# Half as many plain output products between two gating stages, six seven-product groups at the end, and a weight load moved to another queue

## The chip, the cores and the metric

The kernel runs on one core of a Trainium2 chip. The metric is device time in microseconds: the median of several executions on the chip. The engines of the core are TensorE (PE, matrix products; PEld is its weight load), VectorE (DVE), ScalarE (ACT), GpSimd (POOL) and SyncE (SP). SP does nothing here but issue DMAs; ACT issues some too, on a queue of its own. "PSUM bank" below is one of the eight banks of 128×512 f32 in which PE leaves its sums.

## The reference, cut to what matters

Two sub-layers with residuals, on 2048 tokens of width 1024, all in bfloat16:

```python
h  = x + A(layernorm(x))          # segmented attention, 32 heads, 4 segments of 512 tokens
h2 = h + B(layernorm(h))

def B(x, w_in, w_sp, b_sp, w_out):
    z  = gelu(x @ w_in)                            # 2048 x 3584
    z1 = z[..., :1792]
    z2 = layernorm(z[..., 1792:])
    g  = einsum('ts,bsf->btf', w_sp, z2) + b_sp    # mixes tokens: w_sp is 2048 x 2048
    return (z1 * g) @ w_out                        # w_out is 1792 x 1024
```

The change lies in B, behind z1 and z2: in the token mixing ("gating"), the product with `z1`, and the product with `w_out`.

## The kernel before

Every instruction is recorded by a small scheduler, `_Recorder` (L34–241): one list per engine (`pe`, `act`, `dve`, `pool`, `sp`), each in program order, with waits found from the memory cells that an instruction reads and writes. So the order of the Python text is the order on each engine; an engine whose next instruction must wait holds all that stands behind it. All instructions are emitted by one line (`emit`, L210), so a group in the profile is told by its tiles. SBUF is a hand-laid arena (`tens(name, ..., offset)`): two tiles at one address are in use one after the other, and the later waits for the earlier.

The stages, by time in the profiled execution: attention, to about 330 us; z2 = layernorm of the second half of the gelu; z1 to 489.9 (`z1_step`, L1199), kept transposed (features on partitions, tokens along the free axis) in `Z1T`; then four stages that the change touches:

1. `gate(0)` (L1087), 489.9 to 574.6: g and z1·g for tokens 0 to 1023.
2. The w_out units, 574.8 to 623.0: 16 `out_unit`s (L1179). Each makes 128 tokens × 512 columns of the output by 14 matmuls (1792 = 14 × 128) and adds them to `h`, which an earlier stage left in the output's DRAM and `fin_load` brings back.
3. `gate(1)`, 623.0 to 707.8: the same as 1 for tokens 1024 to 2047.
4. The end groups, 707.8 to 753.0: w_out for tokens 1024 to 2047, four groups.

Stages 1, 3 and 4 use a product scheme with seven block products where the plain one has eight (Winograd's form). For gating, w_sp's part is cut in blocks b11, b12, b21, b22, each 512 tokens × 1024; the sums t1 = b12−b11, t2 = b22−t1, t3 = b22−b12, t4 = b21−t2 are made once (`sp_sum`); on the other side four sums of z2 blocks (`s_sum`, tile `ss`, also `SS`) are made for each of the seven feature groups g. One group is seven products of eight matmuls 128×512, in the order t2, t1, b11 of a later group (`p1`), t3, b21 of the next (`p2`), t4, b22. DVE turns the banks into results: `stt` (bank × scale + an addend; tiles `tmp_u`, `tmp_s1b`, `vb`) and `out` (times `Z1T`, into `z1T` or `z1x`). ACT copies p1's bank (`copy1`), POOL adds the row of b_sp to it twice (`tmp_s1b<-tmp_s,brow`). An end group has the same form with seven matmuls per product: `y_sum`s take the place of `s_sum`s, and w_out is cut in 2×2 (the pieces `OB`, sums `ob_sum`).

Scales: the scheme works in f16, so b blocks are multiplied by a power of two, SC[0], when cast from bf16 to f16 (`sp_half` on DVE, a whole block; `sp_part` on ACT, a quarter). The results of gate 1 (Z1X) carry a scale YS, w_out's f16 copies a scale SCW; `scale_y` and `scale_w` work them out among the units from sums of squares, and INVO undoes both.

The preparation of gate 1 lies among the units: 16 DMA transposes on SP's queue (`sp_load`, each 256 KB; tiles `b11r` to `b22r`), the casts, the sums t1 to t4, the first three `ss`. w_out's first half of columns (`WO0`, two DMAs of 896 KB) comes on SP before gate 0; the second half (`WO1`) comes on ACT's queue at the head of the units, beside the transposes. For the end groups the second half comes once more, to `Z1T[:, :, 0:512]`, after the transposes.

Of the kernel before, what the change touches and what calls it, by code (L numbers as in the profile page):

```python
# [33 lines left out]
class _Recorder:  # L34


    def __init__(self, nc):
        self.nc = nc
        self.ops = {k: [] for k in ENGS}
        self.dmas = []  # L40
        self.known = {k: ({f: -1 for f in ENGS}, 0) for k in ENGS}
        self.cells = {}
        self.banks = {}
        self.space = {}
        self.cache = {}
        self.dma_sems = {}
        self.out_dmas = []
        for k in ENGS:
            setattr(self, k, _Eng(self, k))
# [37 lines left out]
    def record(self, eng, name, args, kw, dma=None):  # L87
# [94 lines left out]
        if dma is not None:  # L182
# [4 lines left out]
            key = (aps_out[0] is sb, sb.tensor.name, int(sb.offset))  # L187
# [8 lines left out]
    def emit(self):  # L196
# [9 lines left out]
        def run(eng, e):  # L206
            for op in self.ops[eng]:
                for o in op.waits:
                    e.wait_ge(o.dma if o.dma is not None else sems[o.eng], o.val)
# [49 lines left out]
def bass_sequential_preLN__memory_aug_infini_attn__mixer_gmlp__prompt_kernel(  # L259
# [126 lines left out]
    SQ = b3("sq", [128, 16], F32)  # L386
# [6 lines left out]
    TW, YS, INVY, SCW, INVO = [b3(k, [128, 1], F32) for k in ("tw", "ys", "invy", "scw", "invo")]  # L393
    SQY = tens("sqy", [128, 28], F32, 768)
    BSQ = tens("bsq", [128, 2], F32, 896)
# [6 lines left out]
    WO1 = [tens("w_out1%d" % i, [128, 7, 512], BF16, o * K) for i, o in enumerate((30, 4))]  # L402
    WO0H = [tens("w_out0h%d" % i, [128, 7, 512], F16, o * K) for i, o in enumerate((54, 198))]
    FIN2 = tens("fin2", [128, 4, 2, 2, 512], BF16, 14 * K)
    OT4 = [[tens("ot%d%d" % (i, k), [128, 512], F32, (o + 2 * k) * K) for k in range(4)] for i, o in enumerate((38, 118))]
# [533 lines left out]

    def scale_of(k, n, b):  # L940
# [4 lines left out]
        if k:  # L945
            dve.reciprocal(TOP[:], TOT[:])
        else:
            pool.tensor_tensor(TOP[:], TOT[:], MHZ[:], ALU.pow)
# [53 lines left out]
    at(37, pool.tensor_copy, SQB[:, 0:16], SQ[:])  # L1002
# [6 lines left out]
    at(20, pool.tensor_copy, SQB[:, 0:14], SQZ[:])  # L1009
    at(25, scale_of, 1, 14, None)  # L1010
    at(25, scale_end, 1)
    for k in range(8):
        at(26 + k, wz_half, k // 2, k % 2)
    for k in range(4):
        at(28 + 2 * k, hn_sum, 1, 1 + k // 2, k % 2)
    for k in (1, 2, 3, 4):
        at(35 + k, sz_sum, 0, k)
# [4 lines left out]
    for it in todo:  # L1022
# [6 lines left out]
        if it == (0, 12):  # L1029
            sp_norm_load(0)  # L1030
            sp_norm_load(1)
# [28 lines left out]

    SUMS = {"t1": ("b12", "b11"), "t2": ("b22", "t1"), "t3": ("b22", "b12"), "t4": ("b21", "t2")}
# [25 lines left out]
    def gate(pr, seam=lambda: None, mid=lambda: None, each=lambda g, k: None):  # L1087
        inv, zo = (INV[0], Z1T) if pr == 0 else (INVY, Z1X)
        t1, t2 = slice(1024 * pr, 1024 * pr + 512), slice(1024 * pr + 512, 1024 * pr + 1024)
        s1, s1b1, s1b2, u2, u3 = (TMP[k][:] for k in ("s1", "s1b1", "s1b2", "u2", "u3"))  # L1090

# [19 lines left out]
        def c11(g):  # L1111
            stt(VB[:], g % 3, BROW[0][:])
            out(VB[:], g, 0, t1)
# [6 lines left out]
        if not pr:  # L1120
            p1(2)
        seam()
        p2(0)
        c11(0)
        for g in range(7):
# [6 lines left out]
            ss(4, g)  # L1132
# [3 lines left out]
            if 1 - pr <= g <= 3:  # L1136
                p1(g + 2)
# [12 lines left out]
            stt(VB[:], bc, u3)  # L1150
            out(VB[:], g, 1, t2)
            if not g:
                ss(1, 1)
                ss(2, 1)
            if g < 6:
# [6 lines left out]
            stt(VB[:], bb, s1b1)  # L1162
            out(VB[:], g, 1, t1)
# [3 lines left out]
            stt(VB[:], bc, u2)  # L1167
            out(VB[:], g, 0, t2)
# [10 lines left out]
    def out_unit(u, wsl, q=sp):  # L1179
        tc, lo, w = u  # L1180
        b = next_bank()
        mm8(PS[:, b, 0:w], lambda i: Z1T[:, i, tc * 128:(tc + 1) * 128], wsl, n=14)
        fin = fins[u]
        dve.tensor_tensor(fin[:, 0:w], fin[:, 0:w], PS[:, b, 0:w], ALU.add)
# [7 lines left out]
    wout = B_w_out.rearrange("(c p) n -> p c n", p=128)  # L1192
# [55 lines left out]
    on(1, 7, scale_of, 0, 16, None)  # L1248
    on(2, 2, scale_end, 0)
    for k, g, r in (("b11", 6, 3), ("b12", 6, 3), ("b22", 8, 3), ("b21", 12, 3)):  # L1250
# [17 lines left out]
    units = [(tc, 0, 512) for tc in range(6)] + [(tc, 512, 512) for tc in range(8)] + [(tc, 0, 512) for tc in (6, 7)]  # L1268
# [9 lines left out]
    def z1_norm(g, k):  # L1278
        for h in range(k and 2):
            r, o = 2 * g + (k > 2), 1024 + 512 * h  # L1280
            if k != 2:
                act.activation(bank(7), Z1T[:, r, o:o + 512], ACTF.Square, accum_out=SQY[:, 2 * r + h:2 * r + h + 1])

    gate(0, seam, mid, z1_norm)
    pool.tensor_copy(TW[:], TOT[:])
    fin_load(units[0], act)
    fin_load(units[1], act)
    for k in ("b11", "b12", "b22", "b21"):
        for j in range(4):
            sp_load(1, k, j)  # L1290
    brow_load(1, act)
    for i in range(2):
        act.dma_start(WO1[i][:], wout[:, 7 * i:7 * i + 7, 512:D])
    pool.tensor_copy(SQB[:], SQY[:])

    def total(n):
        b = next_bank()
        pe.matmul(PS[:, b, 0:n], ONES[:], SQB[:, 0:n], start=True, stop=True)
        dve.tensor_reduce(out=TOT[:], in_=PS[:, b, 0:n], axis=mybir.AxisListType.X, op=ALU.add)
        dve.tensor_single_scalar(TOT[:], TOT[:], 1e-30, ALU.max)  # L1300

    def power(o):
        pool.tensor_tensor(TOP[:], TOT[:], MHZ[:], ALU.pow)
        dve.tensor_single_scalar(TOP[:].bitcast(I32), TOP[:].bitcast(I32), 0x7F800000, ALU.bitwise_and)
        dve.tensor_single_scalar(o[:], TOP[:], 8192.0, ALU.mult)

    def scale_y():
        total(28)
        pool.tensor_single_scalar(TW[:], TW[:], float(2 * T * FH), ALU.mult)
        for k in range(2):  # L1310
            pool.tensor_tensor(TW[:], TW[:], BSQ[:, k:k + 1], ALU.add)
        pool.tensor_tensor(TOT[:], TOT[:], TW[:], ALU.mult)
        power(YS)
        dve.tensor_tensor(INVY[:], INV[0][:], YS[:], ALU.mult)
        for k in range(2):
            act.activation(BROW[k][:], BROW[k][:], ACTF.Copy, scale=YS[:])

    def brow_sq():
        for k in range(2):
            act.activation(BH["t4"][:, k, :], BROW[k][:], ACTF.Square, scale=float(np.sqrt(2.0)), accum_out=BSQ[:, k:k + 1])  # L1320

    def wo_norm(k):
        v = (WO0, WO1)[k // 4][k // 2 % 2].rearrange("p c n -> p (c n)")[:, 1792 * (k % 2):1792 * (k % 2) + 1792]
        act.activation(BH["t4"][:, 0:4, :].rearrange("p c n -> p (c n)")[:, 0:1792], v, ACTF.Square, accum_out=SQY[:, k:k + 1])

    def scale_w():
        total(8)
        power(SCW)
        dve.tensor_tensor(INVO[:], YS[:], SCW[:], ALU.mult)
        dve.reciprocal(INVO[:], INVO[:])  # L1330

    for n, u in enumerate(units):
        if n + 2 < 16:
# [3 lines left out]
        if 1 <= n <= 8:  # L1337
            wo_norm(n - 1)
        if n == 6:
            brow_sq()  # L1340
        if n == 7:
            scale_y()
        if n == 10:
            pool.tensor_copy(SQB[:, 0:8], SQY[:, 0:8])
        if n == 1:
            sp_half("b11")
        if n == 4:
            sp_half("b12")
            sp_sum("t1")
        if n == 6:  # L1350
            sp_half("b22")
            sp_sum("t3")
        if n == 8:
            sp_sum("t2")
        if n == 10:
            sp_half("b21")
            sp_sum("t4")
        if n == 12:
# [175 lines left out]
```

## Time and profile before

| | us |
|---|---|
| median of 5 runs | 755.01 (754.09 to 756.37) |
| profiled execution | 754.75 |
| its span in the profile | 753.0 |
| PE busy | 743.7 (99%) |
| DVE busy | 556.9 (74%) |
| ACT busy | 421.7 (56%) |
| POOL busy | 295.7 (39%) |
| gate 0 / units / gate 1 / end groups | 84.7 / 48.4 / 84.8 / 45.2 |

The span is from the first to the last instruction that the profile shows; the execution's time has 1.75 us around it. Matmuls are pipelined, so a row such as "1.89 … x8" is longer than the step from one product to the next; the step is what counts. In the windows view each engine's busy time stands with its number of instructions. A group's row ends with the idle time ahead of it and what released it.

### The profile page before, as it was taken

The page shows a single profiled execution, that of the slowest core. Times are in us where ns is not written, and L with a number is a line of the kernel's source. Part 1 is how long each engine was busy: PE and PEld are TensorE (multiplying, and loading weights), DVE is VectorE, ACT ScalarE, POOL GpSimd, SP SyncE. Part 2 cuts the span into 40 slices and gives each one's busy share as a digit, 9 for nine tenths or more (in the row PEclk, how much of TensorE's full clock was granted, in tenths as well). Part 3 has the DMA queues.
Part 4 walks back from the last instruction along what each step waited for, and adds up shares of the span by engine and source line. Part 5 has one row for each costly group of instructions (what it writes and reads, how often), then busy time and mean ns, then how long its engine had stood idle before and what let it go on. Part 6 is the DMA issues. An engine that isn't in the chain of part 4 may idle for free.

```text
span 753.0 us, 13441 instructions
## 1 busy us (share of the span) xinstructions
PE 743.7 (99%) x5401; PEld 358.8 (48%) x5470; DVE 556.9 (74%) x1013; ACT 421.7 (56%) x519; POOL 295.7 (39%) x450
## 2 busy tenths in 40 slices
PE   8999999999999999999999999999999999999998
PEld 3445455555554445545554444444444444444444
DVE  5586589768975576677986796997885385989776
ACT  6777877787777767325994879733231355300000
POOL 2565456555654334010039888622220001222342
PEclk9999999999999999999999999999999999999999
DMA  9654556444523331669650027330019960001211
GB/s 297 175 166 80 93 82 128 100 78 89 115 67 73 122 88 44 161 183 262 196 164 0 1 45 138 56 98 1 0 26 140 261 203 30 0 1 44 77 50 57
DMA packets 136783, 75.09 MB, mean 100 GB/s; under 512 B 98064, under 2 KB 126480, under 8 KB 136720
## 3 DMA queue, kind: packets, MB, share of 16 engines
q1 hardware_dynamic: 129184, 67.14, 37.0%
q10 hardware_dynamic: 7536, 7.08, 3.5%
q8 instruction: 43, 0.70, 0.4%
q14 instruction: 20, 0.16, 0.1%
HBM read 42.74 MB, written 8.39 MB: 68 GB/s over the span
## 4 chain that ended last, share of the span: by engine, by line
PE 92%; DVE 5%; issue 1%; DMA 1%; ACT 0%; DVEq 0%
PE ps L210 92%; DVE stats L210 1%; DMA wv<-in_A_wv_dram 1%; DVE hch L210 1%; DVE otok L210 1%; DVE pqk L210 0%; DVE lno L210 0%; DVE ta L210 0%; DVE etmp L210 0%; DVE rd L210 0%; DVE rdm L210 0%; DVE mv L210 0%; ACT e L210 0%; ACT L210 0%; DVE upd L210 0%
## 5 line engine op out<-in xcount | busy, mean ns | idle before, releaser
L210 ACT ACTIVATE e<-ps 128x2048 bf16<-128x2048 f32 (+1 forms) x96 | 152.7, 1590 | 41.7 <-PE ps L210 41.5
L210 POOL TENSOR_SCALAR_AFFINE_SELECT e<-e 128x512 bf16<-128x512 bf16 x128 | 90.6, 720 | 131.5 <-ACT e L210 131.5
L210 PE MATMUL ps<-win,hnT 128*128 128x448 bf16 x512 | 98.4, 352 | 0.0
L210 POOL TENSOR_TENSOR tmp_s1b<-tmp_s,brow 128x512 f32<-128x512 f32 x28 | 36.3, 1300 | 121.7 <-DVE tmp_u L210 63.1
L210 PEld LDWEIGHTS ps<-win,hnT 128*128 128x128 bf16 x512 | 49.6, 98 | 46.3 <-issue 0.2
L210 PE MATMUL ps<-wv,xnT 128*128 128x512 bf16 x255 | 59.5, 380 | 1.3 <-DMA wv<-in_A_wv_dram 1.0
L210 PE MATMUL ps<-xnT,wk 128*128 128x512 bf16 x233 | 59.6, 380 | 1.2
L210 DVE TENSOR_TENSOR zt<-ps,zt 128x512 f32<-128x512 f32 x70 | 48.2, 689 | 15.9 <-PE ps L210 12.6
L210 PE MATMUL ps<-wo,oT 128*128 128x512 bf16 x254 | 57.7, 380 | 0.1
L210 PE MATMUL ps<-xnT,wq 128*128 128x512 bf16 x226 | 54.0, 379 | 1.6
L210 ACT ACTIVATE z<-ps 128x448 bf16<-128x448 f32 x60 | 30.6, 544 | 34.9 <-PE ps L210 34.9
L210 PE MATMUL ps<-w_out,z1T 128*128 128x512 bf16 x219 | 48.3, 379 | 0.3
L210 DVE BATCH_NORM_STATS2 zst<-z 128x6 f32<-128x448 bf16 x64 | 38.1, 613 | 10.3 <-ACT z L210 10.2
L210 PEld LDWEIGHTS ps<-v,e 128*128 128x128 bf16 x1280 | 38.8, 96 | 14.0 <-issue 6.5
L210 DVE RECIPROCAL rd<-ps 128x16 f32<-128x16 f32 x32 | 8.0, 250 | 47.1 <-PE ps L210 46.9
L210 PE MATMUL ps<-v,e 128*128 128x33 bf16 x1280 | 42.2, 178 | 0.0
L210 ACT ACTIVATE tmp_s<-ps,invy 128x512 f32<-128x512 f32 x7 | 4.8, 687 | 63.0 <-POOL tmp_s1b L210 36.0
L210 POOL TENSOR_TENSOR sz<-wzh 128x512 f16<-128x512 f16 x28 | 34.8, 1242 | 8.8 <-PE ps L210 8.8
L210 PEld LDWEIGHTS ps<-wo,oT 128*128 128x128 bf16 x256 | 24.1, 98 | 27.6
L210 ACT ACTIVATE z1T<-zt,inv 128x512 bf16<-128x512 f32 x42 | 29.0, 717 | 14.1 <-DVE zt L210 14.1
L210 PEld LDWEIGHTS ps<-xnT,wk 128*128 128x128 bf16 x256 | 22.6, 98 | 29.9 <-issue 5.0
L210 PEld LDWEIGHTS ps<-wv,xnT 128*128 128x128 bf16 x256 | 23.1, 98 | 28.1 <-DMA wv<-in_A_wv_dram 1.6
(204 smaller groups left out, 1456.2 us busy)
## 6 DMA issues: line engine op xcount, KB each, us to landing
sj<-in_B_w_sp_dram SPq DMA_DIRECT2D x16, 512.0 KB, 3.7
xch<-in_A_x_dram SPq DMA_DIRECT2D x16, 256.0 KB, 3.5
xr<-in_A_x_dram SPq DMA_DIRECT2D x16, 256.0 KB, 4.0
out_dram<-hch SPq DMA_DIRECT2D x16, 256.0 KB, 2.4
win<-in_B_w_in_dram SPq DMA_DIRECT2D x4, 896.0 KB, 5.4
wz<-in_B_w_in_dram SPq DMA_DIRECT2D x6, 512.0 KB, 7.6
wo<-in_A_wo_dram SPq DMA_DIRECT2D x1, 2048.0 KB, 8.3
fin<-out_dram ACTq DMA_DIRECT2D x16, 128.0 KB, 2.9
```

Of the source, the lines that this page charges most:

```text
L210: ins = getattr(e, op.name)(*op.args, **op.kw)
```

## The change

**Units and end groups.** The units between the gates are 8 in place of 16: tokens of blocks 0, 4, 1, 5 (of 128), both halves of the columns. The other blocks 2, 6, 3, 7 of the first 1024 tokens join the end groups, which are six in place of four.

**Scale of gate 0.** Since z1·g of tokens 0 to 1023 now also meets the f16 scheme, gate 0 writes the scaled f16 Z1X too. Its scale must be known before gate 0, so it is worked out in the z2 and z1 stages (a load of b_sp, one Square, a POOL power, a few tiny DVE steps); the 28 Squares of z1 in gate 0 give way to 28 Squares of w_out pieces, half of them loaded by 14 DMAs on ACT's queue. `out_unit` multiplies by IY = 1/YS (a `scalar_tensor_tensor` for a `tensor_tensor`).

**Order in the gates.** Gate 0 writes its intermediate values to the f32 tiles u3, s1b1 and u2 in place of the bf16 `vb`. In gate 1 the third p1 comes before the first p2, t4's sums stand in the first group (`mid`), and `ss(4, 0)` and `c11(0)` come later.

**Preparation of gate 1.** b11 is cast on ACT before the units, b21 on DVE after unit 2, b12 on ACT by quarters of columns after units 4 and 5, each followed by its t1 sum on DVE, b22 on ACT after unit 6, its t2 sums after unit 7; then `ss` 1 to 3 and the t3 sums.

**Queues.** SP's order is b11, b21, WO1 (both halves), b12, b22, then w_out's second half again in eight DMAs of 256-byte runs (`ob_load`) in place of one DMA. WO1 was on ACT's queue.

The diff, cut to its core:

```diff
-    WO1 = [tens("w_out1%d" % i, [128, 7, 512], BF16, o * K) for i, o in enumerate((30, 4))]
+    WO1 = [tens("w_out1%d" % i, [128, 7, 512], BF16, o * K) for i, o in enumerate((38, 30))]
...
     def gate(pr, seam=lambda: None, mid=lambda: None, each=lambda g, k: None):
-        inv, zo = (INV[0], Z1T) if pr == 0 else (INVY, Z1X)
+        inv, zo = INVY, Z1X
...
+        c11v, c22v, c21v, c12v = (VB[:],) * 4 if pr else (u3, u3, s1b1, u2)
...
         def c11(g):
-            stt(VB[:], g % 3, BROW[0][:])
-            out(VB[:], g, 0, t1)
+            stt(c11v, g % 3, BROW[0][:])
+            out(c11v, g, 0, t1)
...
         p1(1)
-        if not pr:
-            p1(2)
+        p1(2)
         seam()
         p2(0)
-        c11(0)
+        if not pr:
+            c11(0)
...
             if g == 0:
                 mid()
-            ss(4, g)
+            if g or not pr:
+                ss(4, g)
...
-            if 1 - pr <= g <= 3:
+            if 1 <= g <= 3:
                 p1(g + 2)
...
-            stt(VB[:], bc, u3)
-            out(VB[:], g, 1, t2)
+            stt(c22v, bc, u3)
+            if pr and not g:
+                ss(4, 0)
             if not g:
                 ss(1, 1)
                 ss(2, 1)
+            out(c22v, g, 1, t2)
+            if pr and not g:
+                c11(0)
...
     def out_unit(u, wsl, q=sp):
...
-        mm8(PS[:, b, 0:w], lambda i: Z1T[:, i, tc * 128:(tc + 1) * 128], wsl, n=14)
+        mm8(PS[:, b, 0:w], lambda i: Z1X[:, i, tc * 128:(tc + 1) * 128], wsl, n=14)
...
-        dve.tensor_tensor(fin[:, 0:w], fin[:, 0:w], PS[:, b, 0:w], ALU.add)
+        dve.scalar_tensor_tensor(fin[:, 0:w], PS[:, b, 0:w], IY[:], fin[:, 0:w], ALU.mult, ALU.add)
...
+    def brow_scale():
+        for k in range(2):
+            act.activation(BROW[k][:], BROW[k][:], ACTF.Copy, scale=YS[:])
...
-    units = [(tc, 0, 512) for tc in range(6)] + [(tc, 512, 512) for tc in range(8)] + [(tc, 0, 512) for tc in (6, 7)]
+    units = [(tc, lo, 512) for lo in (0, 512) for tc in (0, 4, 1, 5)]
...
+    def w_norm(g, k):
+        h = 4 * g + k
+        if h % 2:
+            w_sq(14 + h // 2, WOT[:])
+        else:
+            act.dma_start(WOT[:], wout[:, h // 2, 512:D])
+            for c in ([h // 2 - 2] if h >= 4 else []) + ([h // 2] if h >= 24 else []):
+                w_sq(c, WO0[c // 7][:, c % 7, :])
...
-    gate(0, seam, mid, z1_norm)
+    gate(0, seam, mid, w_norm)
+    for u in units[:2]:
+        fin_load(u, act)
+    brow_load(1, act)
-    for k in ("b11", "b12", "b22", "b21"):
+    for k in ("b11", "b21", "b12", "b22"):
+        if k == "b12":
+            for i in range(2):
+                sp.dma_start(WO1[i][:], wout[:, 7 * i:7 * i + 7, 512:D])
         for j in range(4):
             sp_load(1, k, j)
-    brow_load(1, act)
-    for i in range(2):
-        act.dma_start(WO1[i][:], wout[:, 7 * i:7 * i + 7, 512:D])
...
+    for r in range(4):
+        sp_part("b11", r)
     for n, u in enumerate(units):
...
+        w_scale(n)
+        if n == 2:
+            sp_half("b21")
+        if n in (4, 5):
+            for j in (2 * n - 8, 2 * n - 7):
+                sp_cast("b12", j)
+                sp_csum("t1", j)
+        if n == 5:
+            brow_scale()
         if n == 6:
-            brow_sq()
+            for j in range(4):
+                sp_cast("b22", j)
         if n == 7:
-            scale_y()
+            for j in range(4):
+                sp_csum("t2", j)
+    for k in range(1, 4):
+        s_sum(k, 0)
+    for j in range(4):
+        sp_csum("t3", j)
...
+    def ob_load(k):
+        i = 7 if k == "b22" else 0
+        w = wout[:, i:i + 7, 512:D].rearrange("p c (a b t) -> p c a b t", a=2, b=2)
+        o = ob(k, 0, 7, False).rearrange("p (c a) b t -> p c a b t", a=2)
+        for a in range(2):
+            for b in range(2):
+                sp.dma_start(o[:, :, a, b], w[:, :, a, b])
...
-    sp.dma_start(Z1T[:, :, 0:512], wout[:, :, 512:D])
-    gate(1, each=each1)
+    ob_load("b12")
+    ob_load("b22")
+    gate(1, mid=mid, each=each1)
...
+    GR = [(0, 2), (0, 3)] + [(1, j) for j in range(4)]
...
-    for g in range(4):
+    for g in range(6):
         bb, bc = 3 + g % 2, 5 + g % 2
-        last = ((bc, 0, 512),) if g < 3 else ((bc, 0, 384), (7, 384, 512))
+        last = ((bc, 0, 512),) if g < 5 else ((bc, 0, 256), (7, 256, 512))
...
+        if g == 0:
+            for m in range(4):
+                ob_sum("t4", 2 * m)
```

`sp_cast` and `sp_csum` are `sp_part` and a part of `sp_sum` by 128 columns in place of two rows of blocks. `IY`, `YS` and `INVY` are the scale's reciprocal, the scale, and SC's inverse times it.

## The prediction

> **What bounds the kernel now.** I read the page first: busy time, clock row, chain that ended last.
>
> ```profile
> PE 743.7 (99%) x5401; PEld 358.8 (48%) x5470; DVE 556.9 (74%) x1013; ACT 421.7 (56%) x519; POOL 295.7 (39%) x450
> PEclk9999999999999999999999999999999999999999
> PE 92%; DVE 5%; issue 1%; DMA 1%; ACT 0%; DVEq 0%
> ```
>
> PE is busy 99% of the span at full clock, and the chain runs through it. So a removed matmul is time won, and a matmul made to wait is time lost. Then the windows view over the four stages the change touches: gate 0, the w_out units, gate 1, the end groups (stretch, its length, then busy us of PE, PEld, DVE, ACT, POOL; clock, DMA share, GB/s).
>
> ```profile
> 489.90:574.60 84.70, 84.70 (x393) 38.42 (x393) 68.71 (x106) 26.30 (x66) 18.84 (x17) 1.00 0.18 42
> 574.60:623.00 48.40, 48.14 (x222) 21.75 (x226) 26.84 (x38) 17.03 (x22) 1.88 (x6) 1.00 0.92 215
> 623.00:707.80 84.80, 84.80 (x394) 38.29 (x392) 69.69 (x114) 18.23 (x15) 18.07 (x14) 1.00 0.09 29
> 707.80:753.00 45.20, 42.52 (x211) 19.90 (x209) 30.80 (x43) 2.75 (x4) 16.80 (x15) 1.00 0.14 47
> ```
>
> PE has no gap in the first three. In the gates DVE is 81–82% busy, so they are where a longer DVE job can reach PE. The unit stage is where the DMA engines are full (0.92) and DVE is idle for 21.6 us: the preparation of gate 1 is done there. It shrinks to half.
>
> The price of a matmul is read off the PE timeline: eight start every 1.727 us, 0.2159 us each. The units take 623.11 − 574.77 = 48.34 us for 224, the same 0.2158.
>
> ```profile
> 543.47 1.89 PE L210 MATMUL ps<-t2h,ss 128*128 128x512 f16 x8
> 545.20 1.89 PE L210 MATMUL ps<-t1h,ss 128*128 128x512 f16 x8
> 546.92 1.89 PE L210 MATMUL ps<-t3h,ss 128*128 128x512 f16 x8
> 574.77 24.12 PE L210 MATMUL ps<-w_out,z1T 128*128 128x512 bf16 x109
> 623.11 3.62 PE L210 MATMUL ps<-b11h,z2h 128*128 128x512 f16 x16
> ```
>
> **Matmuls.** Removed: 16 units × 14 + 4 groups × 49 = 420. In their place: 8 × 14 + 6 × 49 = 406. 14 × 0.2159 = −3.02 us. One of two small norm matmuls goes: −0.03. The last product is split 256/256 instead of 384/128: the last DVE step takes half of 0.75 instead of a quarter, 0.19 more if a step's time went wholly by its width; I take half of that, +0.1.
>
> **Gate 0.** Its 28 final multiplies read f32 instead of a bf16 `vb`. Before: 0.48. For two f32 inputs the only row is attention's `otok`, mean 0.92, beside POOL.
>
> ```profile
> L210 DVE TENSOR_TENSOR z1T<-vb,z1T 128x512 bf16<-128x512 bf16 x28 | 13.4, 480 | 1.0
> L210 DVE TENSOR_TENSOR otok<-ta,tm 128x512 bf16<-128x512 f32 x24 | 22.1, 923 | 0.3
> L210 DVE TENSOR_TENSOR ss<-z2h 128x1024 f16<-128x1024 f16 x28 | 20.1, 718 | 2.8 <-PE ps L210 2.6
> ```
>
> So between 0 and 0.45 longer each; four per group is up to 1.8 us, against DVE idle of 84.7 − 68.7 = 16 us over seven groups, 2.3 each. The idle is least (about 1) where the loop swaps products, in the fifth group: bounds 0 to +0.8 there, I take +0.2, near the idle side. The 28 Squares on ACT replace 28 Squares; ACT is 26 of 84.7 busy, so they cost nothing; if ACT ran late `copy1` would be next. The 14 extra 128 KB loads ride an 18% busy DMA and cost ACT 14 × 0.45 of issuing, still under half its time.
>
> **Gate 1.** Three sums of w_out pieces fall in its fifth group instead of two (jobs 4,4,4 against 4,4). That group is at the edge now: a `u2` ends at 683.57, and the t4 product, which DVE must not delay, starts at 683.63. One more sum is 0.6; half of it fits elsewhere in the group: +0.33 (bounds 0, 0.7).
>
> ```profile
> 682.83 0.74 DVE L210 SCALAR_TENSOR_TENSOR tmp_u<-ps,invy,tmp_s1b 128x512 f32<-128x512 f32 x1
> 683.63 1.90 PE L210 MATMUL ps<-t4h,z2h 128*128 128x512 f16 x8
> ```
>
> **End groups.** Six instead of four; DVE needs 7.9 of 10.57 us in each by the rows (seven steps of 0.75, four sums of 0.65). The four t4 sums moved into the first end group finish about 1.2 us before their product. No cost; SP's 25 output and 12 input DMAs lie beside PE. The `ob` loads come in 256-byte runs behind b22 on SP, 1.8 MB, landing 601–606 at the rate the transposes show (170–215 GB/s); they are needed after 609, hidden.
>
> **The start of gate 1, the term that decides.** The preparation (b12, b22 casts; t1, t2 sums; three `ss`; t3 sums; t4 sums) was spread over 16 units and done by 623.4. Now it follows, from unit 4 on, one chain in ACT and DVE order. Durations: an ACT cast of a quarter 1.04 start to start, DVE quarter sums 0.6–0.7, unit step 0.75 (scalar form), issue of an out DMA on ACT's queue 0.45.
>
> ```profile
> L210 ACT ACTIVATE b22h<-b22r,sc 128x1024 f16<-128x1024 bf16 x4 | 4.6, 1141 | 0.0
> 587.51 0.45 ACTq L210 DMA_DIRECT2D out_dram<-fin  x1
> 493.42 1.64 DVE L210 TENSOR_TENSOR ss<-z2h 128x1024 f16<-128x1024 f16 x1
> 493.11 2.96 POOL L210 TENSOR_TENSOR tmp_s1b<-tmp_s,brow 128x512 f32<-128x512 f32 x2 [8.19 <-ACT tmp_s L210]
> ```
>
> Unit 4 ends on PE at 574.77 + 5 × 3.02 = 589.9; DVE step 590.8; out issue 591.3 (it stands before the casts on ACT, and waits for the step); casts 0, 1 of b12 to 593.5; sum 594.2; then unit 5's DVE step, queued behind that sum, 594.9; out 595.4; casts 2, 3 and sum 598.3; unit 6's step 599.1, out 599.5; four b22 casts to 603.7; last t2 sum 604.4. PE: units end at 574.77 + 112 × 0.2159 = 598.95; three p1 products to 604.16; p2(0) to 605.9; then t2(0), which needs `ss`. Those sums start at 604.4 and the first two run beside POOL's two adds, as at 493 (1.64 and 1.52 there against 0.68 alone): ready 607.6, PE waits 1.7. After that DVE has from the last t2 sum to the end of the second group's `u2` some 19.8 us in order (`ss` 3.7, t3 2.4, t4 2.4, steps and multiplies of the first group 5.3, the next four `ss` 2.8, two `c11`s 2.45, the `u2` 0.75): until 624.2, with the hand-over 624.4. The t3(1) product overwrites what that `u2` reads and would start at 621.4 with no wait. So PE is late 3.0 in all, which contains the 1.7. Lower bound 0: without the slowing by POOL 1.8 less, and three out issues of 0.45 less if they overlap the casts, as an issue at 595.93 lay inside an ACT step begun at 595.84. Upper 5: the twelve quarter sums of t2, t3, t4 at 0.75, between the single row and t3's mean of 0.92. I take 3.0, what the order of the rows gives. What stands behind a late cast on ACT is the next out issue, and behind a late sum on DVE the next unit's step; both are in the chain.
>
> **WO1 on SP's queue.** Before, both halves were on ACT's queue beside transposes and took 13.8 to 16.5 us (median 15.1); the halves before gate 0, alone on SP, 4.9 to 6.5. PE hid the late landing (a weight load waited 0.30, no matmul).
>
> ```profile
> 576.98 1.23 ACTq L210 DMA_DIRECT2D w_out<-in_B_w_out_dram  x2
> 594.16 4.23 PEld L210 LDWEIGHTS ps<-w_out,z1T 128*128 128x128 bf16 x21 [0.30 <-DMA w_out<-in_B_w_out_dram]
> 577.00:580.00 3.00, 3.00 (x16) 1.35 (x15) 0.69 (x1) 0.00 (x0) 0.00 (x0) 1.00 1.21 85
> 583.00:586.00 3.00, 2.95 (x15) 1.34 (x15) 1.27 (x2) 0.00 (x0) 0.00 (x0) 1.00 1.24 107
> ```
>
> ACT issues two fewer (1.23), and the `fin` load that stood blocked behind them for 8.18 is free. Now it is issued behind b21 at about 576.6, is needed by unit 4 at 586.9, and b12 and b22 queue behind it on SP (landing 590 and 596–599, needed by casts at 591.3 and 599.5). By the SP row plus some 2 us behind b21 and beside `fin` and `brow`: lands 585, margin 1.9, no cost. By the ACT row: 591.7, and b12, b22 later. In between lies that 577–587 moved only 85–158 GB/s with the engines full, which repeated would land WO1 near 589.7: +2.8. I take the SP row, since the queue it now rides is that row's.
>
> The Trainium skill, "DMA: Bandwidth & Descriptors", section "Issuing engines are not separate DMA queues", says that another issuing engine brings no bandwidth of its own, as all share the same 16 engines. The two landings above (4.9–6.5 alone, 13.8–16.5 in company) agree that sharing costs, but no run here changes the queue alone. By that rule WO1 again takes near 15 us and the sum would be about 4.8 us higher (an estimate).
>
> **Sum.** −3.02 − 0.03 + 0.1 + 0.2 + 0.33 + 3.0 = +0.6 against the profiled execution of 754.75 (span 753.0 and 1.75 around it): 755.3. That execution lies 0.26 under the median 755.01, so 755.6.
>
> **Rivals.**
>
> - A, the forecast: the DVE chain at the start of gate 1 eats the gain. 755.6; own range 753.2–757.6. For it: the chain above, DVE 82% busy in the gate. Chance 0.38.
> - B, the gain stays: casts and `ss` sums run faster than rows beside POOL, and the start term vanishes. 755.6 − 3.0 = 752.6. For it: DVE had 21.6 us idle among the units; against: the order puts the work behind the last casts. 0.27.
> - C, the other side: WO1 lands late, because the slow stretch 577–587 comes again. It decides once the first half lands after 586.9; at 589.7 the units stop for 2.8, all that follows shifts: 758.4, and at 591.7 and beyond 760 and more. For it: `brow` and `fin` still run then on ACT's queue; against: ACT's queue no longer carries 1.8 MB beside the transposes. 0.25.
> - D: b22 lands behind WO1 after 599.5, at some 601.5; the cast chain starts 2 later: 757.6. 0.10.
>
> **Range and chances.** A change under 0.2% (1.5 us) can't be told from none. Faster (under 753.5): A 0.06, B 0.25: 0.31. Within: A 0.20, B 0.02, C 0.03, D 0.04: 0.29. Slower: A 0.12, C 0.22, D 0.06: 0.40. From 752.2 (B with the multiplies at nothing) to 759.6 leaves out the low end of B and the high end of C, some 0.18 together.
>
> **What would show it.** Units 112 matmuls without a gap, ending 24.2 after their start; WO1 landing at 585 and no PE wait for `w_out`; PE idle of some 1.7 us ahead of the first t2 product with `ss` as releaser and some 1.3 more ahead of t3 in the second group with `tmp_u`; a gate 1 of about 88 from the first b11 product; end groups of 10.6. A PE wait on `w_out` or on `b12h`/`b22h` whose releaser is a DMA makes C or D right; a gate 1 of 84.8 makes B right. Wrong beyond all these if gate 0 itself grows: seven groups must stay 84.8.

## The result, and the profile after

The changed kernel takes 756.73 us (median of 31 runs, 755.35 to 758.95); the kernel before, in 52 runs, 755.46 (754.07 to 758.21). The ratio is 1.0019, with a 95% interval of 1.0014 to 1.0025: 1.3 us or 0.2% slower. 14 matmuls fewer, worth 3.0 us, have not made it faster.

The profiled execution took 757.62 (span 755.9), 0.9 above its median, where the one of before lay 0.7 below that median. So the two profiles differ by 2.9 where the kernels differ by 1.3; what belongs to the execution and not to the kernel has to be told apart first.

Page of the changed kernel: busy time, clock, and the chain that ended last.

```profile
PE 742.4 (98%) x5388; PEld 357.3 (47%) x5455; DVE 574.5 (76%) x1032; ACT 421.4 (56%) x517; POOL 301.1 (40%) x450
...
PEclk9999999999999999999999999999999999999999
...
PE 75%; DVE 11%; DMA 4%; ACT 4%; POOL 3%; issue 2%; ACTq 0%; DVEq 0%
```

PE is still busy nearly all the time, but the chain no longer runs through it alone: 92% has become 75%, and DVE, DMA and ACT now hold pieces (by its lines some 7% of them, `sj`, `zrs` and `sz`, lie ahead of gate 0). The windows view gives the four stages (the boundaries are the first products of each):

```profile
490.85:575.90 85.05, 85.00 (x394) 38.22 (x393) 76.49 (x106) 26.42 (x66) 17.26 (x15) 1.00 0.23 60
575.90:600.90 25.00, 24.02 (x110) 10.82 (x112) 10.32 (x19) 9.19 (x10) 0.55 (x1) 1.00 1.14 258
600.90:689.30 88.40, 85.45 (x393) 37.94 (x392) 78.42 (x125) 23.07 (x21) 18.72 (x14) 1.00 0.24 59
689.30:755.90 66.60, 63.87 (x309) 29.96 (x307) 46.02 (x68) 4.12 (x6) 22.45 (x18) 1.00 0.16 54
```

Gate 1 has grown from 84.7 to 88.4, and 3 us in it PE is idle. PE's timeline shows the gaps and what ended them (start, length, operation, idle before and its releaser):

```profile
590.34 10.75 PE L217 MATMUL ps<-w_out,z1x 128*128 128x512 bf16 x48 [0.87 <-DMA w_out<-in_B_w_out_dram]
...
607.11 1.90 PE L217 MATMUL ps<-b21h,z2h 128*128 128x512 f16 x8 [0.83 <-ACT tmp_s L217]
...
609.42 1.90 PE L217 MATMUL ps<-t2h,ss 128*128 128x512 f16 x8 [0.42 <-DVE ss L217]
...
614.05 1.90 PE L217 MATMUL ps<-t3h,ss 128*128 128x512 f16 x8 [1.00 <-DVE tmp_u L217]
...
626.74 1.90 PE L217 MATMUL ps<-t3h,ss 128*128 128x512 f16 x8 [0.43 <-DVE tmp_u L217]
...
665.16 1.90 PE L217 MATMUL ps<-t4h,z2h 128*128 128x512 f16 x8 [0.26 <-DVE tmp_u L217]
```

In gate 1 the idle time shown is short of the loss by some 0.16, because a matmul's modelled end lies behind the start that the next could have had; from start to start the six gaps cost 0.85, 1.00, 0.58, 1.16, 0.59 and 0.42. The sum against the profile of before, term by term:

| term | forecast | in the profile |
|---|---|---|
| matmuls (14 big, one small) | −3.05 | −3.05 (112 of the units at 0.2159 make 24.18 of their 25.03) |
| gate 0 | +0.2 | +0.22 (84.83 to 85.05) |
| wait on WO1 among the units | 0 | +0.85 |
| start of gate 1 | +3.0 | +3.33 |
| fifth group of gate 1 | +0.33 | +0.42 |
| end groups | +0.1 | +0.21 |
| ahead of gate 0 | 0 | +0.91 |
| sum | +0.6 | +2.9 |

The forecast was made of the stages from gate 0 on, and there the profile shows +2.0. The medians differ by 1.3 only. The start of gate 0 moves by 2.1 us between the executions below, and of the kernel before there is one profile; where the other 0.7 went stays open.

### The profile page after: what moved, and what is told of

It reads as the page before. It is cut to its first block, busy times and chain, and to the rows that moved or that the text cites. A ratio compares the mean times of both kernels' runs of the same rounds, so it can differ in the third digit from the quotient of the medians.

```text
span 755.9 us, 13436 instructions
## 1 busy us (share of the span) xinstructions
PE 742.4 (98%) x5388; PEld 357.3 (47%) x5455; DVE 574.5 (76%) x1032; ACT 421.4 (56%) x517; POOL 301.1 (40%) x450
## 4 chain that ended last, share of the span: by engine, by line
PE 75%; DVE 11%; DMA 4%; ACT 4%; POOL 3%; issue 2%; ACTq 0%; DVEq 0%
PE ps L217 75%; POOL zrs L217 2%; DMA sj<-in_B_w_sp_dram 2%; ACT sj L217 2%; DVE stats L217 1%; DVE ss L217 1%; POOL sz L217 1%; DMA out_dram<-fin 1%; DMA wv<-in_A_wv_dram 1%; DVE tmp_u L217 1%; DMA fin<-out_dram 1%; DVE hch L217 1%; DVE z1x L217 1%; ACT z L217 1%; ACT b12h L217 1%
## 5 line engine op out<-in xcount | busy, mean ns | idle before, releaser
L217 ACT ACTIVATE tmp_s<-ps,invy 128x512 f32<-128x512 f32 x14 | 9.6, 684 | 90.8 <-POOL tmp_s1b L217 64.7
L217 POOL TENSOR_TENSOR ot<-ot,fin 128x512 f32<-128x512 f32 x18 | 22.4, 1278 | 43.9 <-ACT ot L217 23.4
L217 ACT ACTIVATE ot<-ps,invo 128x512 f32<-128x512 f32 x6 | 4.1, 687 | 61.4 <-PE ps L217 61.4
```

What stands on the lines that cost most here:

```text
L217: ins = getattr(e, op.name)(*op.args, **op.kw)
```

## Experiments

Each one is an edit of the changed kernel. Besides the times, I use a length that the jitter ahead of gate 0 doesn't touch: from the first product of gate 0 to the end of the span ("rest" below; before 263.06, after 265.05).

| run | median us | ratio to before (95%) | rest |
|---|---|---|---|
| c_after | 756.85 | 1.0023 (1.0014–1.0033) | 265.0 |
| e_wo1_act | 762.47 | 1.0100 (1.0085–1.0115) | 270.3 |
| e_wo1_early | 757.24 | 1.0031 (1.0020–1.0042) | 264.8 |
| e_fin8 | 758.96 | 1.0052 (1.0037–1.0068) | 268.5 |
| e_pool_held | 756.86 | 1.0015 (1.0005–1.0025) | 264.9 |
| e_brow_early | 756.78 | 1.0016 (1.0006–1.0025) | 265.1 |
| e_wo1_early_b7 | 757.17 | 1.0017 (1.0007–1.0026) | 265.6 |
| v_early | 761.18 | 1.0066 (1.0045–1.0087) | 270.2 |
| e_no_t3 | 755.56 | 0.9998 (0.9988–1.0007) | 263.0 |
| e_brow_late | 756.76 | 1.0017 (1.0007–1.0026) | 264.1 |
| v_sp | 754.22 | 0.9991 (0.9979–1.0002) | 262.1 |
| v_best | 753.25 | 0.9968 (0.9956–0.9981) | 261.9 |

### The changed kernel again

> The changed kernel once more, unaltered, to see which of its gaps are its own. Theory A (what was read off the one profile is the kernel): z1 again starts about 0.5 later than before's and loses 0.9 up to gate 0, the units stop once for some 0.9 on the second half of w_out, gate 1 is 88.4 long from its first b11 product. Rival (jitter of the DMAs in that one execution): the 0.9 ahead of gate 0 is gone, and the stop among the units moves by more than half a microsecond.

Both theories hold in part. Everything from gate 0 on came back: rest 265.0, the same five waits in gate 1, one stop of 1.01 on WO1. Ahead of gate 0 it did not settle: z1 starts anywhere between 404.57 and 405.89 in the 13 executions of kernels with this same early code (mean 405.2; before, one execution, 405.34), so the late start of z1 is jitter. The z1 stage itself took 84.6 to 85.7 in them (mean 85.0) against 84.60 before, in seven of them with a wait on POOL's `sz` (0.18 to 0.20, once 0.72) that the profile of before does not have; whether the change costs these 0.4 can't be told from one execution of before, and it was not tried alone. Gate 0 takes 85.05 to 85.07 in six of the 13 and 84.83 to 84.85, as before, in seven: its +0.22 is not a fixed cost either.

### WO1 back on ACT's queue

```diff
-        if k == "b12":
-            for i in range(2):
-                sp.dma_start(WO1[i][:], ...)
+    for i in range(2):
+        act.dma_start(WO1[i][:], ...)      # after brow_load, ahead of all sp_load
```

> WO1 goes back to ACT's queue, behind the brow loads; all else as in the changed kernel. Theory A (the queue decides, since on ACT's queue it shares packet by packet with the transposes): it takes 13.8 to 16.5 us again, lands at 592 to 594 against 588 to 590 of the changed kernel, and unit 4, which needs it at 588, stops PE for 3 to 5 us: 2.5 to 4 us slower than the changed kernel. Rival (only bytes and order of arrival matter, since all queues share the engines, and on ACT's queue it is issued a little earlier): it lands within 1 us of the changed kernel's, and the time is the same within 0.7.

5.6 us slower than the changed kernel (c_after, 756.85), more than either theory gave. WO1 was issued 1 us later and took 10.8 to 13.7 us (9.6 to 11.9 on SP's queue), so it landed 2 to 3 us later and not 4; the stops on it are 2.05 and 0.43, and some us at half clock follow (the last section). But the 5.2 by which the rest grew come by another way, which neither theory had: the first b22 cast starts 116.6 after gate 0's first product instead of 111.4, and gate 1's first b21 product waits 2.86.

```profile
589.68 2.89 PE L217 MATMUL ps<-w_out,z1x 128*128 128x512 bf16 x7 [2.05 <-DMA w_out<-in_B_w_out_dram]
...
593.00 10.94 PE L217 MATMUL ps<-w_out,z1x 128*128 128x512 bf16 x48 [0.43 <-DMA w_out<-in_B_w_out_dram]
...
611.98 1.90 PE L217 MATMUL ps<-b21h,z2h 128*128 128x512 f16 x8 [2.86 <-ACT tmp_s L217]
```

The chain that ended last doesn't run through PE here, but through the `fin` buffers (ACT's timeline, then pieces of the chain):

```profile
580.16 4.62 ACTq L217 DMA_DIRECT2D fin<-out_dram  x1
...
584.82 9.02 DMA out_dram<-fin
...
593.86 0.33 ACTq L217
...
594.51 3.47 DMA out_dram<-fin
...
598.00 0.33 ACTq L217
```

Unit 0's result is written out from 584.82, in 9.02, where the changed kernel begins at 580.49 and takes 7.10 (the chain below); the `fin` loads into the buffers, the DVE steps and the casts follow from there.

So the move to SP is worth having, but not because that queue carries more. The Trainium skill, "DMA: Bandwidth & Descriptors", section "Issuing engines are not separate DMA queues", says that the issuing engine brings no bandwidth. The traces agree roughly: the middle of the two landings is 12.2 us on ACT's queue, and on SP's 10.8 in the changed kernel and 8.9 to 12.9 in the other experiments. What the move changes is ACT's own list: with WO1 on ACT's queue the next `fin` load took ACT 4.62 us to issue, and the issue that writes unit 0 out stood behind it.

### WO1 earlier on SP, and the norm matmul's bank

```diff
     for k in ("b11", "b21", "b12", "b22"):
-        if k == "b12": (two WO1 loads)
         for j in range(4):
+            if k == "b21" and j == 3: (two WO1 loads)
             sp_load(1, k, j)
```

> WO1 is issued on SP ahead of the last transposed piece of b21 instead of behind it, about 1.3 us earlier. Theory A (it came late only by its place in the queue): the stop among the units, 0.87, goes, the steps behind it on ACT and DVE come 0.9 earlier, and the time falls by 0.9 to 1. Rival (gate 1 starts on other waits, so that a unit stop is only moved): the stop goes, but gate 1 grows by as much, and the time is within 0.3 of the changed kernel.

WO1 came in time and nothing was won: the units stopped all the same, for 1.53, now because unit 3 needs bank 3, which held the norm matmul's sum.

```profile
584.81 15.28 PE L217 MATMUL ps<-w_out,z1x 128*128 128x512 bf16 x68 [1.53 <-DVE tot L217]
...
607.58 1.90 PE L217 MATMUL ps<-t2h,ss 128*128 128x512 f16 x8 [0.42 <-DVE ss L217]
```

The next run takes that wait away too:

```diff
-            b = 3
+            b = 7
             pe.matmul(PS[:, b, 0:28], ONES[:], SQB[:], start=True, stop=True)
```

> WO1 ahead of the last piece of b21 as before, and the small norm matmul among the units writes bank 7 instead of bank 3, which unit 3 needs. Theory A (with WO1 in time, unit 3 stopped 1.53 only because bank 3 was not read out yet: the reduce stands on DVE behind unit 1's step, and that step waits for a fin load that WO1 delays): no stop among the units, 24.2 long; the wait ahead of b21 comes back in part; in all 0.7 to 1.3 faster than the changed kernel. Rival (the late fin steps hold the casts anyway): units 24.2, but the p2 wait grows by as much, and the time is that of the changed kernel within 0.4.

Now the units run without a stop, 24.21 long, and the rival is right: gate 1 is 89.99 long, its first b21 product waits 2.39 for ACT's copy, and the time is not better. A stop of this size among the units is not the bound; it only decides where PE waits.

### Scaling the b_sp rows earlier

```diff
-        if n == 5:
+        if n == 3:
             brow_scale()
```

> The two brow scalings on ACT (1.32 together), which stand between the b12 and the b22 casts, move to unit 3. Theory A (the b22 casts start when unit 6's DVE step releases the out issue ahead of them, and that step follows the last t1 sum, so ACT has 0.2 to spare there): the wait ahead of the first b21 product in gate 1 falls by 0.2 to 0.5, the time likewise, not to be told from none. Rival (ACT's own load is the chain): the b22 casts come 1.3 earlier, that wait (0.65 to 0.83) goes altogether and part of the 0.42 ahead of t2, the time falls by 1 or more.

1.32 us of ACT work taken from between the casts moved nothing: the first b22 cast starts 111.4 after gate 0's first product (601.32 − 489.95), as in the changed kernel (602.21 − 490.85), and ACT idles 1.82 for DVE instead.

```profile
601.32 2.19 ACT L217 ACTIVATE b22h<-b22r,sc 128x1024 f16<-128x1024 bf16 x2 [1.82 <-DVE fin L217]
...
608.53 1.90 PE L217 MATMUL ps<-t2h,ss 128*128 128x512 f16 x8 [0.42 <-DVE ss L217]
```

In this execution the units stopped longer (26.20), the b21 product did not wait, and the first t2 product started 118.6 after gate 0's first product, as in the changed kernel. That is the pattern of the whole series:

| run | first b22 cast | first t2 product | from cast to t2 | from cast to the end of the span |
|---|---|---|---|---|
| changed kernel | 602.21 | 609.42 | 7.21 | 153.7 |
| e_wo1_early | 600.36 | 607.58 | 7.22 | 153.6 |
| e_brow_early | 601.32 | 608.53 | 7.21 | 153.7 |
| e_wo1_early_b7 | 601.77 | 608.99 | 7.22 | 153.7 |
| e_brow_late | 600.76 | 607.98 | 7.22 | 153.6 |
| e_fin8 | 604.96 | 612.17 | 7.21 | 153.6 |
| e_wo1_act | 607.08 | 614.30 | 7.22 | 153.7 |

Whatever PE waited for ahead of it, the kernel ends 153.7 us after ACT begins to cast b22 (c_after, too). This is the chain: four casts, the last t2 sum, two `ss`, and then DVE's row. A PE wait ahead of it costs only what it delays the casts by. Without any stop, in e_wo1_early_b7, they came no earlier; with the stop of 3.59 in e_fin8, below, they came 3.5 later. In the later kernels with another order (v_early, v_sp, v_best) the b22 casts no longer begin this row, and the distance is another.

### Other ways at the same chain

```diff
...
         copy1(0)
+        if pr:
+            pool.tensor_copy(JNK[:], SS[:, 2, 7, 126:128])
         pool.tensor_tensor(s1b2, s1, BROW[1][:], ALU.add)
```

> At the start of gate 1 POOL's two b_sp adds are held back, by a two-element copy on POOL that reads the third ss sum, until DVE has made the three ss sums; all else as in the changed kernel. Theory A (the chain on DVE from the last t2 sum on is what gate 1 waits for, and POOL beside it makes it 1.8 longer: two ss at 1.5 to 1.6 instead of 0.68): the waits ahead of the first t2 product (0.42 shown idle), the first t3 (1.00) and the second group's t3 (0.43) shrink or go, gate 1 falls from 88.3 to 86.0 to 86.6, the time by 1.7 to 2.3. Rival (the held adds come too late for u2, or the waits belong to the casts ahead and not to DVE's length): gate 1 stays within 0.5 of 88.3.

Gate 1 was 87.58, between the two theories, the time 756.86 and the rest 264.9: no gain, as the rival has it. The `ss` sums ran faster (0.69 and 0.68 instead of 1.53 and 1.64) and the wait ahead of t2 went. But the adds then ran beside the t3 sums, which took 4.40 instead of 2.48; DVE's row was as long as before, the first t3 product waited 1.71 instead of 1.00, and from the first b22 cast to the end it is 153.8. First the t3 sums of the changed kernel, then those of this run and the product's wait:

```profile
610.85 2.48 DVE L217 TENSOR_TENSOR t3h<-b22h,b12h 128x1024 f16<-128x1024 f16 x4
...
607.97 4.40 DVE L217 TENSOR_TENSOR t3h<-b22h,b12h 128x1024 f16<-128x1024 f16 x4
...
613.09 1.90 PE L217 MATMUL ps<-t3h,ss 128*128 128x512 f16 x8 [1.71 <-DVE tmp_u L217]
```

```diff
-    for j in range(4):
-        sp_csum("t3", j)
...
-            prod(bb, SS[:, 2], "t3", False)
+            prod(bb, SS[:, 2], "b12" if pr else "t3", False)
```

> Gate 1's four t3 sums (2.48 on DVE) are left out; its t3 products read the b12 block in their place, so that part of the result is not the reference's, while PE does the same work. Theory A (gate 1 waits for the length of DVE's row behind the last b22 cast): the waits ahead of t3 in the first group (1.16 with its hand-over) and in the second (0.59) go, that ahead of t2 stays, gate 1 falls by 1.7 (to 85.8 to 86.7, depending on the wait ahead of b21), the time by as much. Rival (another wait, PE's or POOL's, stands right behind): gate 1 falls by less than 0.6.

This kernel leaves the four t3 sums out, so part of its result is not the reference's. The wait ahead of the first t3 product went, that ahead of the second shrank from 0.59 to 0.26 (start to start); those ahead of b21 and t2 stayed:

```profile
607.02 1.90 PE L217 MATMUL ps<-b21h,z2h 128*128 128x512 f16 x8 [0.64 <-ACT tmp_s L217]
609.34 1.90 PE L217 MATMUL ps<-t2h,ss 128*128 128x512 f16 x8 [0.42 <-DVE ss L217]
```

Gate 1 fell to 86.72, by 1.5 to 1.7, the rest by 2.0 (the stop on WO1 was shorter too, 0.54), and the distance from the first b22 cast to the end from 153.7 to 152.2. So DVE's row is what PE waits for in the first two groups: made shorter, it moves the end.

```diff
-    FIN = [... for i, o in enumerate((37, 11, 12, 13))]
+    FIN = [... for i, o in enumerate((4, 5, 8, 9, 6, 7, 10, 37))]
...
-    for u in units[:2]:
+    for u in units:
         fin_load(u, act)
```

> All eight fin loads are issued ahead of the units into eight buffers, instead of two ahead of their unit into four that must first be written out. Theory A (unit 4's DVE step at 592.96 waited 1.1 beyond PE for fin, and everything on ACT behind it, the b12 casts first, with it): that step comes at PE's end, the casts 1.1 earlier, gate 1's waits fall from 3.7 to about 2.6, the time by 1.1; the more so as ACT issues less between casts. Rival (the chain is set by the casts and DVE sums themselves, or the 0.8 MB that now come at once push WO1 back): the time stays within 0.4, or the unit stop grows by 0.5 to 2 and takes the gain.

The rival again: WO1, behind 0.8 MB more, was issued at 579.0 and took 11.8 to 14.0, PE stopped 3.59 on it, and the first b22 cast started 3.5 later after gate 0's first product (114.8 instead of 111.4). There PE's wait does count, for the chain that ended last runs from WO1's landing through unit 4's 14 products, at half clock (the last section), to the casts:

```profile
579.03 11.77 DMA w_out<-in_B_w_out_dram
...
590.85 4.93 PE ps L217 x14
...
595.80 0.76 DVE fin L217
```

The first reason, that `fin` is late, is not refuted by it, since WO1 was made late too. The chain of the changed kernel shows it (start, length, what):

```profile
580.49 7.10 DMA out_dram<-fin
587.61 5.26 DMA fin<-out_dram
...
592.96 0.76 DVE fin L217
593.75 0.37 ACTq L217
...
594.16 2.20 ACT b12h L217 x2
```

A buffer of unit 0 is written out in 7.10, unit 4's `fin` is loaded into it in 5.26, unit 4's DVE step follows, then its out issue on ACT, and only then the casts of b12, although PE had been done with unit 4 at 591.9.

```diff
-    brow_load(1, act)
...
         w_scale(n)
+        if n == 3:
+            brow_load(1, act)
```

> The two brow loads on ACT's queue, 128 KB each by broadcast, go out at unit 3 instead of ahead of the units. Theory A (the broadcast beside the transposes is what makes the transfers at the head of the units slow, as the slow stretch of the kernel before began with it): WO1 lands in 7 to 8 us instead of 9.6 to 12, the stop on it (0.9 to 1.7) goes, fin comes earlier too, the time falls by 0.9 to 1.5. Rival (0.25 MB are just bytes among 6 MB): WO1 lands at most 1 us earlier, and the time falls by less than 0.6.

WO1 landed in 7.9 to 10.8 instead of 9.6 to 11.9, the units did not stop, the casts came 0.9 earlier and the rest fell by 1.0; by the times (ratio 1.0017 against 1.0023) the gain can't be told from none. The broadcast may slow its neighbours somewhat (one execution); most of the transfers' length is there without it.

### The preparation moved ahead

```diff
-    for k in ("b11", "b21", "b12", "b22"):
-        if k == "b12":
+    for k in ("b11", "b12", "b22", "b21"):
+        if k == "b22":
             (two WO1 loads)
...
+        if n in (5, 6): (two b22 casts and t2 sums)
+        if n == 7: (t3 sums, b21's cast)
         out_unit(...)
+        if n in (1, 2): (two b12 casts and t1 sums)
+        if n == 3: brow_scale()
...
```

> The preparation of gate 1 moved ahead: SP's order is b11, b12, WO1, b22, b21; the b12 casts and t1 sums stand at units 1 and 2, the brow scalings at 3, the b22 casts and t2 sums ahead of the steps of units 5 and 6, the t3 sums and b21's cast ahead of the step of unit 7; only the three ss are left behind the units; the norm matmul in bank 7. Same work, no piece left out. Theory A (the gain of 3.05 on the matmuls was eaten by the chain behind the last casts and by the stop on WO1): gate 1 85.0 to 85.6 long, units 24.2 to 24.6, the time 752.0 to 753.0, some 4 below the changed kernel and 2 to 3 below before. Rival (the DMA engines are the limit of the shorter unit stage: 6 MB at 260 GB/s are 23 us whatever the order): b22 or b21 land after 600, the waits only change their names, and the time stays above 755.

761.18, wrong by 8. Units 24.20, but the first b21 product waited 6.32 for ACT's copy. ACT's timeline shows why:

```profile
598.11 2.19 ACT L217 ACTIVATE b22h<-b22r,sc 128x1024 f16<-128x1024 bf16 x2 [2.77 <-DMA out_dram<-fin]
...
602.13 2.19 ACT L217 ACTIVATE b22h<-b22r,sc 128x1024 f16<-128x1024 bf16 x2 [1.83 <-DVE fin L217]
...
605.74 4.60 ACTq L217 DMA_DIRECT2D out_dram<-fin  x2
...
610.39 0.69 ACT L217 ACTIVATE tmp_s<-ps,invy 128x512 f32<-128x512 f32 x1 [6.07 <-DVE fin L217]
```

The casts stood behind a `fin` load that waited for its buffer, and gate 1's copy behind the out issues of units 6 and 7; the DVE step of unit 7 I had put behind the t3 sums and b21's cast. A cast is ready when its block has landed; on ACT's list it waited for everything before it. So in the next version the outs of units 3 to 7 go to SP's queue:

```diff
-        out_unit(u, ..., act)
+        out_unit(u, ..., act if n < 3 else sp)
...
-    FIN = [... (37, 11, 12, 13)]
+    FIN = [... (37, 12, 13, 10, 11, 9)]
...
+        if n in (5, 6): (b22 casts and t2 sums, behind the unit's step)
...
+    s_sum(1, 0); s_sum(2, 0); sp_half("b21"); s_sum(3, 0)
```

> As v_early, with ACT's list freed of late DMAs: the out DMAs of units 3 to 7 are issued on SP behind the block loads, fin has six buffers in place of four, the b22 casts stand behind the units' steps, b21's cast behind the second ss. Same work. Theory A (v_early failed because ACT, in order, held the b22 casts and gate 1's first copy behind out and fin DMAs): b22 casts from 593 to 598, no wait of ACT's copy, p2 waits for b21's landing at most 1; gate 1 85.0 to 86.2, units 24.2, the time 752.0 to 753.5, faster than before. Rival (the DMA engines cannot bring b12, WO1, b22, b21, fin and brow, some 6 MB, in the 29 us from 576 to 605): the wait ahead of the first b21 product stays above 1.5 with a landing behind it, and the time is above 755.

754.22, 2.5 below the changed kernel (the rest by 2.9), but above the 752.0 to 753.5 of theory A, and by the ratio not to be told from the kernel before. The first b22 cast now starts 102.1 after gate 0's first product instead of 111.4 and waits for nothing but its block. Gate 1 is 85.90. The version changes order, queue and buffers together; what each gives was not tried.

```profile
591.71 1.15 ACT L217 ACTIVATE b22h<-b22r,sc 128x1024 f16<-128x1024 bf16 x1 [1.81 <-DMA b22r<-in_B_w_sp_dram]
...
605.11 1.90 PE L217 MATMUL ps<-b21h,z2h 128*128 128x512 f16 x8 [0.41 <-DVE b21h L217]
```

The last version removes two of the three waits left:

```diff
-    s_sum(1, 0); s_sum(2, 0); sp_half("b21"); s_sum(3, 0)
+    for j in range(4):
+        sp_cast("b21", j)
+    for k in range(1, 4):
+        s_sum(k, 0)
...
-    (2, 2, 2, 3, 3, 3, 3, 4, 4, 4, 5, 6)
+    (2, 2, 2, 3, 3, 3, 3, 4, 4, 5, 5, 6)
```

> As v_sp, with b21's cast in four column quarters on ACT behind the b22 casts instead of one DVE instruction beside POOL (2.19), and one t3 piece of w_out moved from gate 1's fifth group to its sixth. Same work. Theory A (v_sp's two waits left in gate 1 are b21's cast, 0.99 with its hand-over, and DVE's load in the fifth group, 0.42): both go, gate 1 is 84.6 to 85.0 long, the time 0.9 to 1.4 under v_sp's 754.2, and clearly faster than before: ratio 0.9965 to 0.998. Rival (b21's last piece lands at 602 and its cast holds ACT's first copy, or the piece moved makes the sixth group wait): gate 1 stays at 85.6 or more, the time within 0.4 of v_sp's.

753.25, a ratio of 0.9968 (0.9956 to 0.9981): faster than both kernels, though by 0.3% only. PE's timeline shows no idle time in gate 1; its length is 84.99. The page shows the chain running through PE again:

```profile
PE 741.8 (99%) x5388; PEld 357.5 (48%) x5455; DVE 572.2 (76%) x1031; ACT 426.4 (57%) x521; POOL 300.7 (40%) x450
...
PE 90%; DVE 5%; DMA 3%; issue 1%; SPq 1%; ACT 0%
```

On PE's timeline the stop among the units is left:

```profile
589.47 10.75 PE L217 MATMUL ps<-w_out,z1x 128*128 128x512 bf16 x48 [1.19 <-DMA w_out<-in_B_w_out_dram]
```

It is 1.19 long, and the chain that ended last now runs from this load (13.46) into PE's products, so it should count in full; this was not tried.

## Why the prediction was right, point by point

The forecast, case A, gave 755.6 with a range of 752.2 to 759.6 and put the gain's loss at the start of gate 1. The median is 756.73, the difference to before +1.3 where the sum said +0.6; it stays under the 1.5 that the prediction took for the least that can be told from none, and such an outcome had 0.29. The rest, which the sum was about, grew by 2.0; that the medians lie nearer to the forecast is luck, as nothing in the sum accounts for the 0.7 between them. The mechanism is the one forecast: e_no_t3 and the table of b22 casts show that gate 1 waits for the row of casts and sums, and in v_best, where that row is moved ahead, 2.1 of the 3.0 us of the matmuls come back by the medians, 1.1 by the rest.

- *Matmuls, gate 0, fifth group, end groups*: −3.05, +0.22, +0.42, +0.21 against −3.05, +0.2, +0.33, +0.1. Near in size, but not all for the reason given. The fifth group is: v_best moves one sum out of it and the wait goes. Gate 0's +0.22 is missing in seven of 13 executions. In the end groups the split of the last product, forecast at +0.1, costs nothing (from its start to the end of the span 4.29, before 4.37); instead the first t4 product, forecast at no cost, starts 0.30 late behind DVE's four t4 sums (3.17) and the step after them:

```profile
697.83 3.17 DVE L217 TENSOR_TENSOR z2h<-w_out0h,z2h 128x1024 f16<-128x1024 f16 x4
700.93 0.74 DVE L217 SCALAR_TENSOR_TENSOR ot<-ps,invo,ot 128x512 f32<-128x512 f32 x1
...
701.73 1.68 PE L217 MATMUL ps<-z2h,z1x 128*128 128x512 f16 x7
```

- *Start of gate 1, 3.0*: 3.33 in gate 1, but PE had by then already stood 0.85 in the units, and both belong to one delay: 4.2. The step that was off is "Unit 4 ends on PE ... DVE step 590.8". Gate 0 ended 1.13 later in the profiled execution than in the one of before, so the step should have come at about 591.9; it ended at 593.7. 0.85 of that is WO1, 1.0 is unit 4's `fin`, whose buffer had first to be written out. From the first b22 cast on the row was right: forecast 4.9 to the last t2 sum (599.5 to 604.4), measured 5.0 (602.21 to 607.2); forecast 19.8 from there to the second group's `u2`, measured 19.5 (607.2 to 626.7). Where the waits showed was partly wrong: 1.7 was expected ahead of t2 and 1.3 ahead of the second t3; they were spread over the first b21 product (1.00), t2 (0.58) and both t3 (1.16, 0.59). "Three p1 products ... p2(0) to 605.9" overlooked that ACT's copy of the first p1 stands behind the b22 casts.
- *WO1 on SP's queue, no cost*: wrong in the landing (9.6 to 11.9 us, not about 8, nor the near 15 of the other estimate) and in the stop (0.85 to 1.0, not 0), which is case C at a third of its price. It made no difference on its own: case C's sum added the stop to the chain, and the b7 run shows that without the stop the wait reappears in gate 1. The slow stretch did not come again with WO1 on SP: 151 GB/s at the least between 577 and 587 (by stretches of 2 us), where it had been 85 to 158.
- *Rival B*, the gain stays: refuted for the changed kernel. *Rival D*, late b22: its last piece was issued only at 598.7 and took at least 4.3, so it did land late, but it was not waited for: it was cast at 605.3, one step behind the cast before it.
- *"What would show it"*: units "without a gap" was wrong, gate 1 of about 88 and end groups of 10.6 were right.

The part of the difference that the two profiles show ahead of gate 0 (0.9) was not in the sum. Nothing here shows more than jitter for half of it; the other half is open.

## What to carry to other kernels

When a stage is shortened, add up what else was hidden in it before counting the gain: here 24 us of units went, and with them the cover for the casts, sums and loads of the next stage. An engine whose list holds both computations and DMA issues can hand a late transfer on to its next computation, as ACT did here (6.07 in v_early); look for the DMA issue that stands ahead of work whose data are already there. And if removing a wait moves the time by nothing, look for a start-to-end distance that stays the same over the runs: it names the chain, and shortening the chain tests it.

## What the runs showed that was not expected

PE's clock fell after pauses of only two to two and a half microseconds. In e_wo1_early_b7 PE idled 2.39 up to 606.67; the windows view (PE's clock is the third number from the end) shows full clock for about another microsecond, half clock for some 3 us, and full clock again:

```profile
606.00:606.60 0.60, 0.00 (x0) 0.00 (x0) 0.53 (x1) 0.60 (x3) 0.00 (x0) 1.00 1.32 264
...
607.00:608.00 1.00, 1.00 (x6) 0.39 (x4) 0.96 (x2) 1.00 (x1) 1.00 (x1) 0.95 1.39 226
608.00:609.00 1.00, 1.00 (x4) 0.17 (x3) 1.00 (x2) 0.51 (x1) 1.00 (x2) 0.50 1.29 213
...
610.00:611.00 1.00, 1.00 (x4) 0.30 (x2) 1.00 (x2) 1.00 (x2) 0.00 (x0) 0.50 0.06 16
611.00:612.00 1.00, 1.00 (x5) 0.45 (x4) 1.00 (x3) 1.00 (x1) 0.00 (x0) 0.85 0.00 0
```

The same came after 2.05 (e_wo1_act), 3.59 (e_fin8) and 6.32 (v_early), where the clock was 0.50 to 0.54 in the next window, but not after 2.86 (e_wo1_act, later) nor after any of the pauses of up to 1.71 (e_pool_held). The Trainium skill, "TensorE: Matmul & The Clock Gate", section "HAM oscillation — how this bites in real kernels", gives about 3.4 us of idle time as the limit; two of these runs lost the clock below that, and one at 2.86 did not, so the length of the pause alone does not decide it. Some 3 us at half clock do the work of 1.5, so such a pause takes 1.5 us of PE's time beside its own length. Whether the kernel pays for it depends on the chain: in e_wo1_early_b7 it fell behind the b22 casts, and the distance from them to the end is the same 153.7 as without it; in e_fin8 unit 4's 14 products lay on the chain, and took 4.93 instead of 3.02.
